# Dilated-window attention with a two-layer feed-forward: token tiles of 512, a first batch normalised after its values, and another activation sequence

## The chip, the cores and the metric

The kernel runs on one core of a Trainium2 chip. The metric is the device time of one execution in microseconds. Three runs of the kernel before gave a median of 971.6 us (lowest 970.74). The profile describes one further execution. Its engines are PE (TensorE matmul), PEld (its weight load), DVE (VectorE), ACT (ScalarE), POOL (GpSimd) and SP, which issues the DMAs.

## The reference

Eight batches of eight heads, 576 positions, head dimension 64. Heads 0 to 3 of a batch attend to the last 32 positions, heads 4 to 7 to every fourth of the last 128. The result, as 4608 tokens of 512 features, goes through two matrices with a piecewise activation between them.

```python
rel = pos[:, None] - pos[None, :]
mask_plain = (rel >= 0) & (rel < 32)
mask_dil = (rel >= 0) & (rel < 128) & (rel % 4 == 0)
scores = np.where(mask, q @ k.T / 8, -1e9); scores -= scores.max(-1)
attn = np.exp(scores); attn = attn / (attn.sum(-1) + 1e-09)
x = (attn @ v)            # to (4608, 512)
h = x @ w_in              # 512 x 2048
g = np.where(h >= 1, h, np.where(h <= -1, 0.0, (h + 1) ** 2 / 4))
out = g @ w_out           # 2048 x 512
```

## The kernel before, in words

**Precision.** Matmuls of the feed-forward run on single-pass operands. Each factor is split into a high part and a remainder (`xh`, `xl`; `gh`, `gl`; the two halves of `wi[f]`, `wo[f]`), and three products are added. The weights arrive as 64-bit words; `weights` (line 105) turns a block into its two parts with two ACT operations, one or two DVE operations, an ACT copy and a POOL subtraction. There are 16 blocks `wi` and 16 `wo`.

**Attention.** The host reorders the dilated heads so that every head is a band: six query tiles of 96 against 128 keys each. `scores` (line 169) and `scores_split` (line 198) make the scores, `reduce` (line 156) adds the mask and takes the row minimum of the negated scores, `softmax` (line 230) takes six exponentials with their sums, makes the reciprocals and multiplies on POOL. The probabilities are transposed by TensorE (`transpose_pe`, line 274; batches 0 and 1) or DVE (`transpose`, line 249; later), and `values` (line 303) multiplies two heads with their values; `store_x` (line 296) splits the result into `xh` and `xl`. Batches 0 and 1 (16 heads) take the scores in full precision ("native"); the other 48 heads use split operands (`split`, line 131).

**Feed-forward.** Tokens are cut into 12 tiles of 384. A step is one pair (token tile t, block f of 128 hidden features): `layer1` (line 345) runs 12 matmuls of 384 columns into the PSUM tile `h`, then lines 365 to 372 make `gh` and `gl`: ACT's half-and-relu, DVE's min-and-square, DVE's max with `h`, ACT's copy, and a subtraction on DVE (on POOL in the first 11 blocks). `layer2` (line 377) follows two steps later with 9 matmuls of 512 columns into three accumulators; after f = 15 they are copied and stored.

**Order.** The order of TensorE's instructions is written out by hand (line 529); on the other engines, SP's queue among them, a list scheduler orders the work by program order and simulated readiness. First come batch 0's scores, transposes and values, then a quarter of five layer-1 blocks (`partial`), then the steps. During the steps of tile 0, which this text calls the first pass, the weights are converted two blocks ahead (line 555) and `units` of batch 1's attention are put between the blocks. From step 16 on, `plan_rest` (line 408) puts a pair of heads into every six steps. PSUM has eight banks: three `acc`, two `h`, three `att`. The x tiles have four buffers each.

**Transfers.** All DMAs go through SP's queue: queries and keys of a native pair in four transfers, values one head at a time, weights at once, up to line 536.

Of the kernel before, what the change touches and what calls it, by code (L numbers as in the profile page):

```python
# [30 lines left out]
TOK = 384  # L32
# [8 lines left out]
def body(ctx, tc, q, k, v, mask, eye, w_in, w_out, out):  # L41
# [9 lines left out]
    half_t = const.tile([128, 16], F32, name="half_t")[:, :1]  # L51
# [3 lines left out]
    heads = {}  # L55

# [5 lines left out]
    def load_pair(n):  # L62

        b, h = divmod(n, H)
        if 0 < n < H:
            qr, kr = borrow(f"qr{n}")[:, :S], borrow(f"kr{n}")[:, :KPAD]
        else:
            tags = ("qs", "kk") if n % 4 else ("qr", "kr")
            qr = pool.tile([128, S], F32, tag=tags[0], name=f"qr{n}")
            kr = pool.tile([128, KPAD], F32, tag=tags[1], name=f"kr{n}")  # L70
        for j in range(2):
            r = slice(64 * j, 64 * j + 64)
            nc.sync.dma_start(out=qr[r], in_=q[b, h + j, :64])
            nc.sync.dma_start(out=kr[r], in_=k[b, h + j, :64])
            heads[n + j] = dict(qs=qr[r], ks=kr[r])

    def load(n):
        b, h = divmod(n, H)
        qr = pool.tile([128, S], F32, tag="qr", name=f"qr{n}")
        kr = pool.tile([128, KPAD], F32, tag="kr", name=f"kr{n}")  # L80
        nc.sync.dma_start(out=qr, in_=q[b, h])
        nc.sync.dma_start(out=kr, in_=k[b, h])
        heads[n] = dict(qr=qr, kr=kr)

    def load_values(n):
        if 0 < n < H:
            both = borrow(f"vt{n}")[:, : 2 * NQ * D].rearrange("p (j t d) -> p j t d", j=2, t=NQ)
        for j in range(2):
            if 0 < n < H:
                vt = both[:, j]  # L90
            else:
                vt = pool.tile([128, NQ, D], F32, tag="vt", name=f"vt{n + j}", bufs=3)
            b, h = divmod(n + j, H)
            nc.sync.dma_start(out=vt, in_=v[b, h])
            heads[n + j]["vt"] = vt
# [9 lines left out]
    def weights(f, w, name):  # L105
# [9 lines left out]
        if name == "wi":  # L115
# [12 lines left out]
        nc.scalar.copy(out=w[f][:, 0], in_=mf)  # L128
# [16 lines left out]
    banks = [("acc0", 1), ("acc1", 1), ("acc2", 1), ("h", 2), ("h", 2)]  # L145
# [10 lines left out]
    def reduce(n, t, parts):  # L156

        nc.vector.tensor_tensor_reduce(  # L158
# [10 lines left out]
    def scores(n, t0, t1):  # L169

        hd = heads[n]
        plain = n % H < H // 2
        if t0 == 0:
            begin(n)
        if n < H:
            tag, bufs = banks[(2 * n + t0 // 4) % len(banks)]
        else:
            tag, bufs = "att", 3
        sp = ps.tile([128, 512], F32, tag=tag, name=f"s{n}_{t0}", bufs=bufs)
        sv = sp[:QT, : (t1 - t0) * 128].rearrange("p (t j) -> p t j", j=128)  # L180
        if n == 0 and t0 == 0:

            half = half_t.broadcast_to([128, 128])
            for _ in range(11):
                PE.matmul(out=sp[:, :128], lhsT=half, rhs=half, start=True, stop=True)
        for t in range(t0, t1):
            PE.matmul(
                out=sv[:, t - t0],
                lhsT=hd["qs"][:, t * QT : (t + 1) * QT],
                rhs=hd["ks"][:, t * QT : t * QT + 128],  # L190
                start=True,
                stop=True,
            )
        for t in range(t0, t1):
            which = (0 if t == 0 else 2) if plain else t % 3
            reduce(n, t, (sv[:, t - t0], msk[:, which]))

    def scores_split(n, t0):
# [6 lines left out]
        sp = ps.tile([128, 512], F32, tag="att", name=f"s{n}_{t0}", bufs=3)  # L205
# [42 lines left out]

    def transpose(n):
# [9 lines left out]

    def borrow_pts():  # L260

        for i in range(2):
            for part in ("xh", "xl"):
                both = pool.tile([128, NC * TOK], F32, tag=part, name=f"pts_{part}{i}", bufs=4)
                for j in range(2):
                    pt = both[:, j * NQ * QT : (j + 1) * NQ * QT]
                    first_pts.append(pt.rearrange("p (t j) -> p t j", j=QT))

    first_pts = []

    def pt_of(n):
        return first_pts[n] if n < H else pts[n % 2]

    def transpose_pe(n):
        pt, c = pt_of(n), heads[n]["c"]
        for t0, t1 in ((0, 4), (4, NQ)):
            tag, bufs = banks[(2 * n + t0 // 4) % len(banks)] if n < H else ("att", 3)
# [5 lines left out]

    xt = {}

    def xtile(t):
        if t not in xt:
            xt[t] = (
                pool.tile([128, NC, TOK], F32R, tag="xh", name=f"xh{t}", bufs=4),
                pool.tile([128, NC, TOK], F32R, tag="xl", name=f"xl{t}", bufs=4),  # L290
# [3 lines left out]
    last = {}  # L294

    def store_x(src, t, c, dst):
        xh, xl = xtile(t)
        nc.scalar.copy(out=dst(xh[:, c]), in_=src)
        last["x"] = nc.vector.tensor_tensor(
# [3 lines left out]
    def values(n, part):  # L303
# [3 lines left out]
        odd = b % 2  # L307
        first = (2 if odd else 4) if plain else 3
        t0, t1 = ((0, first), (first, NQ))[part]
        op = ps.tile([128, 512], F32, tag="att", name=f"o{n}_{part}", bufs=3)  # L310
        for j in range(2):
            for t in range(t0, t1):
                PE.matmul(  # L313
                    out=op[64 * j : 64 * j + 64, (t - t0) * QT : (t - t0 + 1) * QT],
                    lhsT=heads[n + j]["vt"][:, t],
                    rhs=pt_of(n + j)[:, t],
# [3 lines left out]
        c = h // 2  # L320
        tok0 = b * S
        if plain:
            w = (t1 - t0) * QT
            tok = tok0 + t0 * QT
            t, at = divmod(tok, TOK)
            store_x(op[:, :w], t, c, lambda x: x[:, at : at + w])
        else:
            cut = CLS * (TOK // 2 if odd else TOK) // S
            for a, z in ((0, cut), (cut, CLS)):
                t, at = divmod(tok0 + DIL * a, TOK)  # L330
                store_x(
                    op[:, : 2 * CLS].rearrange("p (r i) -> p r i", r=2)[:, :, a:z],
                    t,
                    c,
                    lambda x: x[:, at : at + DIL * (z - a)].rearrange("p (i r) -> p r i", r=DIL)[
                        :, 2 * part : 2 * part + 2
                    ],
                )
# [6 lines left out]
    def layer1(t, f, cs=range(NC), bank=("h", 2)):  # L345
        xh, xl = xtile(t)
        if cs[0] == 0:
            hps[t, f] = ps.tile([128, 512], F32, tag=bank[0], name=f"h{t}_{f}", bufs=bank[1])[:, :TOK]
# [13 lines left out]
        y = pool.tile([128, TOK], F32, tag="y", name=f"y{t}_{f}", bufs=2)  # L362
        gh = pool.tile([128, TOK], F32R, tag="gh", name=f"gh{t}_{f}", bufs=3)
        gl = pool.tile([128, TOK], F32R, tag="gl", name=f"gl{t}_{f}", bufs=3)
        nc.scalar.activation(out=y, in_=hp, func=AF.Relu, bias=half_t, scale=0.5)  # L365
        nc.vector.scalar_tensor_tensor(out=y, in0=y, scalar=1.0, in1=y, op0=ALU.min, op1=ALU.mult)  # L366
        activated = nc.vector.tensor_tensor(out=y, in0=hp, in1=y, op=ALU.max)  # L367
        if t == 0:
            last["g", f] = activated
        nc.scalar.copy(out=gh, in_=y)  # L370
        low = nc.gpsimd if t == 0 and f < 11 else nc.vector
        low.tensor_tensor(out=gl, in0=y, in1=gh.bitcast(F32), op=ALU.subtract)  # L372
# [4 lines left out]
    def layer2(t, f):  # L377
        gh, gl = gs.pop((t, f))
        for m in range(TOK // 128):
# [12 lines left out]
            if f == NF - 1:  # L392
                o = pool.tile([128, DM], F32, tag="m", name=f"out{t}_{m}", bufs=3)
                if m == 1:
# [6 lines left out]
    nhead = B * H  # L401
    native = 2 * H

    units = []
# [3 lines left out]
    def plan_rest():  # L408

        pattern = [("0", "1"), ("2", "VW"), ("", ""), ("T3", "4"), ("5", ""), ("U", "")]  # L410

        def after(m):
            if m < nhead - 1:
                split(m + 1)
            if m < nhead - 2:
                load(m + 2)
            softmax(m)

        for p in range((nhead - native) // 2 + 1):
            n = native + 2 * p  # L420
            ops = {"V": [lambda n=n: values(n - 2, 0)], "W": [lambda n=n: values(n - 2, 1)]}
            if n < nhead:
                for j in range(2):
                    for i, u in enumerate(score_units(n + j, after)):
                        ops[str(3 * j + i)] = [u]
                ops["T"] = [lambda n=n: (transpose(n), load_values(n))]
                ops["U"] = [lambda n=n: transpose(n + 1)]
            for i, (a, b) in enumerate(pattern):
                if p == 0 and i < 3:
                    continue  # L430
                s = NF + 6 * p + i - 3
                lists = slots.setdefault(s, ([], []))
                for names, l in ((a, lists[0]), (b, lists[1])):
                    for x in names:
                        if not (p == 0 and x in "VW012"):
                            l.extend(ops.get(x, []))

    def score_units(m, after):
# [207 lines left out]
```

## Time and profile before

| quantity | value |
|---|---|
| median of three runs | 971.6 us |
| the profiled execution's own time | 971.83 us |
| its span, first to last instruction | 969.0 us |
| mean granted TensorE clock | 0.988 |
| DMA, HBM read and written | 63.49 MB, 9.44 MB |

The 2.8 us between span and time lie outside the instructions. In a group's row the columns are line, engine, operation, output from inputs, shape and count; then busy time, mean duration of one, idle time of the engine ahead of it and what ended that. A full-precision matmul has two rows in the trace, so the 48 score matmuls of batch 0 count as 96. Rows in order of time give start, duration and count.

### The profile page before, as it was taken

Reading aid. Unit: us, or ns where it says so; the run is one execution under the profiler, and the core shown is the slowest. Engines: PE = TensorE matmul, PEld = TensorE weight load, DVE = VectorE, ACT = ScalarE, POOL = GpSimd, SP = SyncE. Lnnn points to the kernel's source line nnn. Section 1 sums busy time; section 2 is a strip of 40 time slices with the busy share of each in tenths; the row PEclk is TensorE's granted clock in tenths of the full one; section 3 lists DMA queues with packets and bytes.
Section 4 is the critical chain, followed back from the end, with each engine's and each line's share of the span. In section 5 each row is a group of like instructions: output and inputs, shape, how many; then the busy total and the mean of one; then the engine's idle time right before and its main releaser. Section 6 shows DMA issues by size and latency. Waiting matters only on the chain.

```text
span 969.0 us, 15838 instructions
## 1 busy us (share of the span) xinstructions
PE 938.7 (97%) x5398; PEld 842.2 (87%) x5398; DVE 710.9 (73%) x1922; ACT 536.0 (55%) x1609; POOL 423.3 (44%) x375
## 2 busy tenths in 40 slices
PE   8779989999999999999999999999999999999998
PEld 7667768998999899999889999989899988999997
DVE  5688998878777877877787877788777777444433
ACT  6988666555565555556555545654654564322322
POOL 2566665545554554455455445545544552000000
PEclk8899999999999999999999999999999999999999
DMA  8991113213212211321222222212312310000000
GB/s 257 358 353 42 42 43 99 57 53 100 68 36 90 67 55 55 100 67 43 83 68 62 79 68 67 77 49 67 92 50 68 100 34 1 33 1 1 33 1 32
DMA packets 35888, 73.95 MB, mean 76 GB/s; under 512 B 4288, under 2 KB 12768, under 8 KB 35808
## 3 DMA queue, kind: packets, MB, share of 16 engines
q1 hardware_dynamic: 35808, 72.95, 24.1%
q8 instruction: 42, 0.69, 0.3%
q14 instruction: 38, 0.31, 0.1%
HBM read 63.49 MB, written 9.44 MB: 75 GB/s over the span
## 4 chain that ended last, share of the span: by engine, by line
PE 73%; DVE 12%; ACT 7%; DMA 4%; SPq 2%; POOL 2%; issue 1%; POOLq 0%; DVEq 0%; ACTq 0%
PE h L352 34%; PE acc L385 33%; DVE y L366 3%; PE s L208 3%; PE o L313 3%; ACT c L233 3%; DMA wi_raw<-w_in 2%; DVE pt L255 2%; DVE wo_m L123 2%; DVE y L367 1%; DMA kr<-k_in 1%; DVE gl L372 1%; ACT gh L370 1%; DVE c L241 1%; ACT y L365 1%
## 5 line engine op out<-in xcount | busy, mean ns | idle before, releaser
L352 PE MATMUL h<-xh,wi 128*128 128x384 f32 x1536 | 431.5, 342 | 6.1 <-DVE y L367 5.1
L385 PE MATMUL acc<-wo,gh 128*128 128x512 f32 x1152 | 390.1, 393 | 3.0 <-DVE out L395 3.0
L352 PEld LDWEIGHTS h<-xh,wi 128*128 128x128 f32 x1536 | 282.7, 189 | 15.7 <-DVE y L367 5.3
L352 PE MATMUL h<-xl,wi 128*128 128x384 f32 x768 | 259.7, 338 | 0.0
L385 PEld LDWEIGHTS acc<-wo,gh 128*128 128x128 f32 x1152 | 216.8, 188 | 45.0 <-DVE out L395 4.3
L370 ACT CAST gh<-y 128x384 fp32r<-128x384 f32 x192 | 98.4, 512 | 270.8 <-DVE y L367 270.8
L226 POOL TENSOR_TENSOR c<-c,msk 96x256 f32<-96x256 f32 (+1 forms) x168 | 116.6, 700 | 300.8 <-ACT c L216 300.5
L385 PE MATMUL acc<-wo,gl 128*128 128x512 f32 x576 | 225.9, 392 | 0.0
L366 DVE SCALAR_TENSOR_TENSOR y<-y 128x384 f32<-128x384 f32 x192 | 137.4, 716 | 73.5 <-ACT y L365 72.7
L365 ACT ACTIVATE y<-h,half_t 128x384 f32<-128x384 f32 x192 | 111.2, 579 | 114.8 <-PE h L352 114.1
L372 DVE TENSOR_TENSOR gl<-y,gh 128x384 fp32r<-128x384 f32 x181 | 120.9, 668 | 53.8 <-ACT gh L370 52.1
L233 ACT ACTIVATE c<-c 96x128 f32<-96x128 f32 x384 | 151.3, 397 | 13.3 <-DVE c L158 12.7
L352 PEld LDWEIGHTS h<-xl,wi 128*128 128x128 f32 x768 | 144.9, 189 | 4.1
L255 DVE STREAM_TRANSPOSE pt<-c 32x192 f32<-32x192 f32 x288 | 106.1, 368 | 24.7 <-POOL c L245 20.6
L385 PEld LDWEIGHTS acc<-wo,gl 128*128 128x128 f32 x576 | 108.4, 188 | 15.6 <-POOL gl L372 0.2
L245 POOL TENSOR_TENSOR c<-c 96x768 f32<-96x768 f32 x64 | 98.4, 1537 | 50.1 <-DVE c L244 43.8
L158 DVE CUSTOM_DVE_ANT_0 c<-s,c 96x128 f32<-96x128 f32 x288 | 73.1, 283 | 61.2 <-POOL c L226 56.0
L367 DVE TENSOR_TENSOR y<-h,y 128x384 f32<-128x384 f32 x192 | 107.1, 558 | 6.5
L140 POOL TENSOR_TENSOR kk<-kr,kk 128x608 fp32r<-128x608 f32 x48 | 81.5, 1698 | 3.8
L137 POOL TENSOR_TENSOR qs<-qr,qs 64x576 fp32r<-64x576 f32 x48 | 71.2, 1482 | 5.9 <-issue 2.3
L233 ACT ACTIVATION_READ_ACCUMULATOR c<-c 96x1 f32 x384 | 73.3, 191 | 0.0
L241 DVE SCALAR_TENSOR_TENSOR c<-c 96x6 f32<-96x6 f32 x64 | 62.4, 976 | 7.0 <-ACT c L233 5.9
(47 smaller groups left out, 726.7 us busy)
## 6 DMA issues: line engine op xcount, KB each, us to landing
kr<-k_in SPq DMA_DIRECT2D x48, 304.0 KB, 3.1
qr<-q_in SPq DMA_DIRECT2D x48, 288.0 KB, 2.8
vt<-v_in SPq DMA_DIRECT2D x64, 192.0 KB, 3.0
out<-out SPq DMA_DIRECT2D x36, 256.0 KB, 2.1
wi_raw<-w_in SPq DMA_DIRECT2D x16, 512.0 KB, 9.2
wo_raw<-w_in SPq DMA_DIRECT2D x16, 512.0 KB, 10.2
kr<-k_in SPq DMA_DIRECT2D x16, 152.0 KB, 4.0
qr<-q_in SPq DMA_DIRECT2D x16, 144.0 KB, 3.9
```

Source lines behind the costliest of these rows:

```text
L140: nc.gpsimd.tensor_tensor(out=kk[:, 1], in0=hd["kr"], in1=kk[:, 0].bitcast(F32), op=ALU.subtract)
L226: nc.gpsimd.tensor_tensor(out=c[:, ts], in0=c[:, ts], in1=m, op=ALU.add)
L233: nc.scalar.activation(out=c[:, t], in_=c[:, t], func=AF.Exp, bias=st[:, 0, t : t + 1], scale=-1.0, accum_out=st[:, 1, t : t + 1],)
L245: nc.gpsimd.tensor_tensor(out=c, in0=c, in1=st[:, 2].unsqueeze(2).broadcast_to([QT, NQ, 128]), op=ALU.mult)
L255: nc.vector.transpose(out=pt[r : r + 32, :, 32 * g : 32 * g + 32], in_=c[32 * g : 32 * g + 32, :, r : r + 32],)
L352: PE.matmul(out=hp, lhsT=wi[f][:, w, 128 * c : 128 * c + 128], rhs=x[:, c], start=c == 0 and i == 0, stop=c == NC - 1 and i == len(terms) - 1,
L365: nc.scalar.activation(out=y, in_=hp, func=AF.Relu, bias=half_t, scale=0.5)
L366: nc.vector.scalar_tensor_tensor(out=y, in0=y, scalar=1.0, in1=y, op0=ALU.min, op1=ALU.mult)
L367: activated = nc.vector.tensor_tensor(out=y, in0=hp, in1=y, op=ALU.max)
L370: nc.scalar.copy(out=gh, in_=y)
L372: low.tensor_tensor(out=gl, in0=y, in1=gh.bitcast(F32), op=ALU.subtract)
L385: PE.matmul(out=acc[m], lhsT=g[:, r], rhs=wo[f][:, w], start=f == 0 and i == 0, stop=f == NF - 1 and i == len(terms) - 1,)
```

## The change

- `TOK` is 512: 9 token tiles, 144 steps, 12 + 12 matmuls of 512 columns per step. PSUM is now four `acc`, two `h`, two `att`; batch 0 also uses the four `acc` banks by turns. The x tiles have three buffers.
- The activation is a DVE clamp of `h` to [-1, 1], an ACT square of (y + 1) / 2, a DVE max written back into `h`, an ACT copy of `h` to `gh` and a DVE subtraction from `h`; `y` has one buffer, `gh` and `gl` two.
- Batch 0 takes no sums with its exponentials. POOL subtracts the minima, ACT takes one exponential per head, and in `values` TensorE sums the transposed probabilities against a column of ones, DVE makes the reciprocals, TensorE spreads them over 64 partitions (a matmul with the identity), ACT copies them out and DVE multiplies them in.
- The scores of two native heads are made alternately, one from partitions 0 to 63 and the other from 64 to 127.
- The first four `wi` blocks and `wo` 0 are converted with DVE in place of ACT for part of the work.
- Queries, keys and values of a native pair come in one transfer each; weight blocks are fetched four (`wo`) and six (`wi`) steps ahead. SP's queue is in program order too.
- The hand-written order is one table of half steps (`slots`): a native pair every seven half steps, from head 16 on a pair every eight (four steps). The third score set of a split head directly follows the second.

```diff
-TOK = 384
+TOK = 512
...
+    banks = [("acc0", 1), ("acc1", 1), ("acc2", 1), ("acc3", 1)]
...
+        for t in range(t0, t1):
+            for m, sv in zip(pair, svs):
+                PE.matmul(
+                    out=sv[:, t - t0],
+                    lhsT=heads[m]["qs"][:, t * QT : (t + 1) * QT],
...
+    def exponentials(n):
+        least = st[:, 0].unsqueeze(2).broadcast_to([QT, NQ, 128])
+        nc.gpsimd.tensor_tensor(out=c, in0=c, in1=least, op=ALU.subtract)
+        last["act"] = nc.scalar.activation(out=c, in_=c, func=AF.Exp, scale=-1.0)
...
+        if n < H:
+            for i in range(2 * NQ):
+                PE.matmul(
+                    out=sums[:, i : i + 1],
+                    lhsT=pt_of(n + i // NQ)[:, i % NQ],
+                    rhs=one_t,
...
+            nc.vector.tensor_scalar(out=inv, in0=sums, scalar1=EPS, scalar2=None, op0=ALU.add)
+            nc.vector.reciprocal(out=inv, in_=inv)
+        for part in range(2):
+            op = ps.tile([128, 512], F32, tag="att", name=f"o{n}_{part}", bufs=2)
...
+                        PE.matmul(
+                            out=sc[64 * j : 64 * j + 64, i * QT : (i + 1) * QT],
+                            lhsT=inv[:, at : at + 1].broadcast_to([QT, 64]),
+                            rhs=ident,
...
+                nc.scalar.copy(out=over, in_=sc[:, w])
+                nc.vector.tensor_tensor(out=op[:, w], in0=op[:, w], in1=over, op=ALU.mult)
...
-        nc.scalar.activation(out=y, in_=hp, func=AF.Relu, bias=half_t, scale=0.5)
-        nc.vector.scalar_tensor_tensor(out=y, in0=y, scalar=1.0, in1=y, op0=ALU.min, op1=ALU.mult)
-        activated = nc.vector.tensor_tensor(out=y, in0=hp, in1=y, op=ALU.max)
-        nc.scalar.copy(out=gh, in_=y)
-        low = nc.gpsimd if t == 0 and f < 11 else nc.vector
-        low.tensor_tensor(out=gl, in0=y, in1=gh.bitcast(F32), op=ALU.subtract)
+        nc.vector.tensor_scalar(
+            out=y, in0=hp, scalar1=-1.0, scalar2=1.0, op0=ALU.max, op1=ALU.min
+        )
+        nc.scalar.activation(out=y, in_=y, func=AF.Square, bias=half_t, scale=0.5)
+        activated = nc.vector.tensor_tensor(out=hp, in0=hp, in1=y, op=ALU.max)
+        copied = nc.scalar.copy(out=gh, in_=hp)
+        nc.vector.tensor_tensor(out=gl, in0=hp, in1=gh.bitcast(F32), op=ALU.subtract)
...
+    for n in range(H, native, 2):
+        u = 7 * (n - H) // 2
+        place(u, lambda n=n: scores_pair(n, 0, 4))
+        place(u + 1, lambda n=n: (scores_pair(n, 4, NQ), after_pair(n)))
+        place(u + 5, lambda n=n: transpose_pe(n))
+        place(u + 6, lambda n=n: transpose_pe(n + 1))
+        place(u + 7, lambda n=n: values_native(n))
+    for n in range(native, nhead, 2):
+        u = 27 + 4 * (n - native)
+        for j, at in ((0, u), (1, u + 4)):
+            place(at, lambda m=n + j: scores_split(m, 0))
+            place(at + 1, lambda m=n + j: scores_split(m, 2))
+            place(at + 1, lambda m=n + j: (scores_split(m, 4), after(m)))
+        place(u + 4, lambda n=n: (transpose(n), load_values(n)))
+        place(u + 8, lambda n=n: transpose(n + 1))
+        place(u + 11, lambda n=n: values(n))
...
+            if s + 6 < NF:
+                fetch(s + 6, w_in, "wi")
+            if s + 4 < NF:
+                fetch(s + 4, w_out, "wo")
+            if 0 < s < NF:
+                todo = [("wo", s, False)]
+                if s + 3 < NF:
+                    todo.append(("wi", s + 3, False))
+                behind(last["g", max(s - 2, 0)], *todo)
+            if s < 2:
+                layer1(*steps[s], range(2, NC))
+            elif s < len(steps):
+                layer1(*steps[s])
+            run(2 * s)
+            while l2 <= s - lag and l2 < len(steps):
+                layer2(*steps[l2])
+                l2 += 1
+            run(2 * s + 1)
```

More of the change, by code (lines that the diff above doesn't have):

```diff
@@ L40, in body @@
 @with_exitstack
-def body(ctx, tc, q, k, v, mask, eye, w_in, w_out, out):
+def body(ctx, tc, q, k, q2, k2, v, mask, eye, w_in, w_out, out):
     nc = tc.nc
@@ L62, in load_pair @@
     def load_pair(n):
-        b, h = divmod(n, H)
         if 0 < n < H:
@@ L114, in weights @@
         )
-        if name == "wi":
+        if name == "wi" and not on_vector:
             top = raw.bitcast(U8).rearrange("p (n x) -> p n x", x=8)[:, :, 3]
@@ L167, in reduce, with scores_pair @@
         )
-    def scores(n, t0, t1):
-        hd = heads[n]
+    def scores_pair(n, t0, t1):
+        pair = (n, n + 1)
         plain = n % H < H // 2
[L173 to L185, printed above, removed]
-        for t in range(t0, t1):
[L187 to L196, printed above, removed]
+        svs = []
+        for m in pair:
+            if t0 == 0:
+                begin(m)
+            tag, bufs = bank(n)
+            sp = ps.tile([128, 512], F32, tag=tag, name=f"s{m}_{t0}", bufs=bufs)
+            svs.append(sp[:QT, : (t1 - t0) * 128].rearrange("p (t j) -> p t j", j=128))
+            if m == 0 and t0 == 0:
+                half = half_t.broadcast_to([128, 128])
+                for _ in range(11):
+                    PE.matmul(out=sp[:, :128], lhsT=half, rhs=half, start=True, stop=True)
+        for t in range(t0, t1):
+            for m, sv in zip(pair, svs):
+                PE.matmul(
+                    out=sv[:, t - t0],
+                    lhsT=heads[m]["qs"][:, t * QT : (t + 1) * QT],
+                    rhs=heads[m]["ks"][:, t * QT : t * QT + 128],
+                    start=True,
+                    stop=True,
+                )
+        for m, sv in zip(pair, svs):
+            for t in range(t0, t1):
+                which = (0 if t == 0 else 2) if plain else t % 3
+                reduce(m, t, (sv[:, t - t0], msk[:, which]))
     def scores_split(n, t0):
@@ L204, in scores_split @@
         c = hd["c"]
-        sp = ps.tile([128, 512], F32, tag="att", name=f"s{n}_{t0}", bufs=3)
+        sp = ps.tile([128, 512], F32, tag="att", name=f"s{n}_{t0}", bufs=2)
         sv = sp[:QT].rearrange("p (t a j) -> p t a j", t=2, a=2)
@@ L258, in transpose @@
                 )
+    first_pts = []
     def borrow_pts():
[L262 to L269, printed above, removed]
+        for part in ("xh", "xl"):
+            both = pool.tile([128, NC * TOK], F32, tag=part, name=f"pts_{part}", bufs=3)
+            for j in range(3):
+                pt = both[:, j * NQ * QT : (j + 1) * NQ * QT]
+                first_pts.append(pt.rearrange("p (t j) -> p t j", j=QT))
     def pt_of(n):
-        return first_pts[n] if n < H else pts[n % 2]
+        return first_pts[n] if n < len(first_pts) else pts[n % 2]
     def transpose_pe(n):
@@ L319, in values @@
                 )
[L320 to L338, printed above, removed]
+            inv = heads[n + 1]["st"].rearrange("p k t -> p (k t)")[:, NQ:]
```

324 lines of the change are left out of this document (148 added, 176 removed).

## The prediction

> **What bounds the kernel now.** I read the page first, then the busy time by stage, then TensorE's waits, then its rows in order of time.
>
> ```profile
> PE 938.7 (97%) x5398; PEld 842.2 (87%) x5398; DVE 710.9 (73%) x1922; ACT 536.0 (55%) x1609; POOL 423.3 (44%) x375
> PE   8779989999999999999999999999999999999998
> PEclk8899999999999999999999999999999999999999
> ```
>
> TensorE is 97% busy; its only thin slices are the first five or six, where the granted clock is lower too. Busy time by stage separates them:
>
> ```profile
> 0.00:51.00 51.00, 41.10 (x301) 37.25 (x302) 31.61 (x145) 40.53 (x143) 21.05 (x20) 0.83 0.96 313
> 51.00:162.00 111.00, 97.34 (x580) 82.29 (x579) 97.95 (x239) 82.07 (x239) 72.51 (x56) 0.97 0.32 104
> 162.00:966.00 804.00, 800.28 (x4521) 722.66 (x4519) 581.32 (x1539) 413.44 (x1229) 329.71 (x301) 1.00 0.19 57
> ```
>
> (Columns: stage, length, then PE, PEld, DVE, ACT, POOL, clock, DMA.) There are three regimes: the start (batch 0's attention; ACT 40.5 of 51 us), the first pass (16 blocks of the first token tile, with 32 weight conversions and batch 1's attention; DVE 98 of 111), and the rest, where PE is busy 800 of 804. The rest can only shrink by shorter matmul streams; the first two by moving work off DVE and ACT, or by giving their idle PE more to do. After 150 us PE's waits hold one line:
>
> ```profile
> PE acc L385 <- DVE out L395: 3.0, 3, 1.2
> ```
>
> **The matmul stream.** In the undisturbed tail one step is twelve 384-column matmuls, then nine of 512:
>
> ```profile
> 861.18 0.34 PE L352 MATMUL h<-xh,wi 128*128 128x384 f32 x1
> ...
> 863.28 0.40 PE L385 MATMUL acc<-wo,gh 128*128 128x512 f32 x1
> ...
> 865.34 0.34 PE L352 MATMUL h<-xh,wi 128*128 128x384 f32 x1
> ```
>
> From start to start: 2.10 us / 12 = 0.175 us for 384 columns, 2.06 / 9 = 0.229 for 512. The extra 128 columns cost 0.054, so 384 should cost 0.162 if there were no fixed part; each matmul carries some 13 ns. With 512 tokens a step is twelve and twelve: 24 x 0.2285 = 5.48 us, and there are 144 steps for 192. Layer 1 falls from 192 x 2.10 = 403 to 144 x 2.74 = 395; layer 2 keeps its 1728 matmuls. That alone is 8 us.
>
> "TensorE: Matmul & The Clock Gate" in the Trainium skill, section "Back-to-back issue gap", gives an isolated warm matmul N/2.4 + 2.5 ns: 162.5 ns for 384 and 216 for 512, and by it the saving would be 1.5 us, an estimate that speaks against the change. The rows show 175 and 229, so I keep mine.
>
> **The rest of the kernel.** I cut at the end of layer 2's block 15, the row at 161.24:
>
> ```profile
> 161.24 0.34 PE L352 MATMUL h<-xh,wi 128*128 128x384 f32 x1
> ...
> 964.87 0.39 PE L385 MATMUL acc<-wo,gh 128*128 128x512 f32 x1
> ```
>
> From there to 965.2 are 804 us, in them 174 layer-1 blocks and 176 of layer 2: 365 + 363 = 728. The other 76 us are attention of heads 17 to 63 and its seams. After the change 126 + 128 blocks remain, 254 x 2.74 = 696; with the same 76 and 4 us of tail, the span ends **776 us after that cut**. So every extra token of the first pass is work moved ahead of the cut, into a regime where PE had idle time.
>
> Do the other engines keep up? Per block the change has clamp, square, max, copy, subtract, on 512 columns:
>
> ```profile
> L366 DVE SCALAR_TENSOR_TENSOR y<-y 128x384 f32<-128x384 f32 x27 | 15.1, 560 | 50.4 <-ACT y L365 50.4
> L367 DVE TENSOR_TENSOR y<-h,y 128x384 f32<-128x384 f32 x26 | 14.5, 558 | 0.9
> ...
> L395 DVE COPY out<-acc 128x512 f32<-128x512 f32 x1 | 0.7, 680 | 0.0
> ```
>
> (DVE in the tail.) A 512-column DVE operation out of PSUM takes 0.68; three are 2.05 us per 5.48 us step, where three of 0.56 stood per 4.16. A DVE write into PSUM (the new max) is in no row; I bound it by 0.56 (this max at 384 columns) and 1.36, twice the copy, and take 0.69 as nearest to the copy. At 1.36 DVE would still have room. On ACT:
>
> ```profile
> L397 ACT COPY out<-acc 128x512 f32<-128x512 f32 x24 | 13.8, 587 | 3.4 <-PE acc L385 3.2
> L128 ACT CAST wi<-wi_m 128x512 fp32r<-128x512 f32 x16 | 9.9, 628 | 2.8 <-DVE wi_m L123 2.5
> ```
>
> square 0.63 and copy 0.59. The chain from a finished h to gl is 0.68 + 0.63 + 0.69 + 0.59 + 0.68, some 3.5 us with hand-overs. h now stays held through the subtract, but its next writer comes three blocks (8.2 us) later; gh's second buffer is free one block (2.7 us) after the step, when the copy is due anyway. Both hide behind PE's stream; without that cover each microsecond late would cost 144 us in all. Pairs of heads now come every four steps (22 us of GEMM) in place of six (25), so attention is denser, but DVE's share per pair falls with the activation.
>
> The scores are the tight spot: "att" has two buffers in place of three, and the third score set of a head follows the first after one block and one set, 2.74 + 0.24 = 3.0 us. Before:
>
> ```profile
> 407.49 0.40 PE L208 MATMUL s<-kk,qs 128*96 128x256 f32 x2
> ```
> ```profile
> 408.58 0.35 ACT L216 COPY c<-s 96x256 f32<-96x256 f32 x1
> ```
> ```profile
> 409.01 0.99 POOL L226 TENSOR_TENSOR c<-c,msk 96x256 f32<-96x256 f32 x1 [3.41 <-ACT c L216]
> ```
> ```profile
> 411.14 0.28 DVE L158 CUSTOM_DVE_ANT_0 c<-s,c 96x128 f32<-96x128 f32 x1
> ```
>
> That set was read out 3.9 us after its issue, of which waiting in ACT's queue took some 0.7 and in DVE's, behind an activation, 0.9. In the new order the set starts when the block's subtract is nearly through and before the next clamp, so I expect about 2.3 us and no wait; bounds 0 and 0.9 us for 47 heads, 0 to 42 us. I take 0, and put the far end with a rival.
>
> **The first pass.** What DVE did in it:
>
> ```profile
> L366 DVE SCALAR_TENSOR_TENSOR y<-y 128x384 f32<-128x384 f32 x18 | 28.0, 1557 | 5.4 <-ACT y L365 5.3
> L123 DVE SCALAR_TENSOR_TENSOR wo_m<-wo_m,wo_raw 128x512 uint32<-128x512 uint32 x13 | 18.5, 1424 | 0.0
> ...
> L367 DVE TENSOR_TENSOR y<-h,y 128x384 f32<-128x384 f32 x18 | 10.0, 557 | 0.6
> ...
> L372 DVE TENSOR_TENSOR gl<-y,gh 128x384 fp32r<-128x384 f32 x6 | 4.6, 759 | 0.2 <-ACT gh L370 0.2
> ```
>
> The reader is to see 1557 against 560 ns: the same instruction, all of whose operands lie in SBUF, takes nearly three times as long here, where POOL is busy 72 of 111 us, while the max, which reads PSUM, takes 557 in both places. The change gives each of the three an operand in PSUM. DVE's activation falls from 28.0 + 10.0 + 4.6 = 42.6 to 18 x 3 x 0.69 = 37 us although the tile is a third larger and eleven subtractions come over from POOL. So DVE needs 98 - 42.6 + 37 = 92 us, and with 5 for weight conversions that now fall later about 97.
>
> PE's need from two finished layer-1 blocks to the cut: 16 + 16 blocks x 2.74 = 88; batch 1's attention by
>
> ```profile
> 98.23 1.55 PE L187 MATMUL s<-kr,qr 64*96 64x128 f32 x12
> 99.71 0.45 PE L352 MATMUL h<-xh,wi 128*128 128x384 f32 x1
> ...
> 89.41 1.59 PE L313 MATMUL o<-pt,vt 128*64 128x96 f32 x24
> 90.93 0.44 PE L352 MATMUL h<-xh,wi 128*128 128x384 f32 x1
> ```
>
> 96 score rows x 0.123 = 12, 96 value rows x 0.063 = 6, transposes and head 16 some 6. The new order alternates two heads that lie in different halves of the partitions; no row shows whether their matmuls overlap. I bound the scores by 12 and, at the value rows' pitch, 6 us, and take 12: **112 us**. By "TensorEngine Tiling (Array Packing)" of the Trainium skill, "Key Properties", tiles on separate row groups run in parallel, so the scores would take half and the forecast would be 6 us lower; no run here shows it.
>
> Before, PE had 91 us of work in the 111 us after 50.4: 20 us of waits. With DVE at 97 of 117 (it was 98 of 111) and PE the fuller engine, I take 5 us of waits, bounds 2 and 20.
>
> **The start.** Batch 0 now subtracts the minimum on POOL, takes one exponential per head, sums on TensorE and scales after the values.
>
> ```profile
> L233 ACT ACTIVATE c<-c 96x128 f32<-96x128 f32 x384 | 151.3, 397 | 13.3 <-DVE c L158 12.7
> L245 POOL TENSOR_TENSOR c<-c 96x768 f32<-96x768 f32 x64 | 98.4, 1537 | 50.1 <-DVE c L244 43.8 <-ACT wo_m L112 2.1 <-DVE c L158 1.2
> L136 ACT CAST kk<-kr 128x608 fp32r<-128x608 f32 x48 | 33.7, 701 | 0.0
> L158 DVE CUSTOM_DVE_ANT_0 c<-s,msk 96x128 f32<-96x128 f32 x96 | 21.5, 278 | 9.0 <-PE s L187 9.0
> ```
>
> ACT loses 48 exponentials (151.3 / 384 = 0.39 each, 19 us) and gains eight wide ones (0.85 each by the 608-column cast) and eight copies of 288 columns (0.38 each by the score copy's 0.35 for 256): 9 us less. DVE gains eight multiplies, at most 0.56 each by the 384-column max, and loses four pairs of small operations; those 4 us lie under its idle time (31.6 of 51 busy). POOL's subtractions follow the reductions; the last of eight ends near 9.4 + 8 x 1.5 = 21 us, and the last exponential at 22, where the last normalisation came here:
>
> ```profile
> 30.61 1.47 POOL L245 TENSOR_TENSOR c<-c 96x768 f32<-96x768 f32 x1 [1.16 <-DVE c L244]
> ```
> ```profile
> 7.24 0.29 DVE L158 CUSTOM_DVE_ANT_0 c<-s,msk 96x128 f32<-96x128 f32 x1 [6.37 <-PE s L187]
> ```
> ```profile
> 30.13 0.71 PE L280 MATMUL t<-ident,c 96*128 96x96 f32 x6
> ...
> 50.05 0.34 PE L352 MATMUL h<-xh,wi 128*128 128x384 f32 x1
> ```
> ```profile
> wi_raw<-w_in SPq DMA_DIRECT2D x16, 512.0 KB, 9.2
> wo_raw<-w_in SPq DMA_DIRECT2D x16, 512.0 KB, 10.2
> ```
>
> That stall goes, and PE is late next: 24 more matmuls per pair, 48 rows x 0.063 = 3 us, 12 in all, with each scale waiting for DVE's reciprocal; DVE's reductions start at 7.2 as before, behind the warm-up matmuls, and take 21.5 / 96 = 0.22 each. From the end of the reductions (7.2 + 48 x 0.22 = 17.8): transposes 6.5 (48 rows at 0.12, and hand-over), four values-with-sums at 4.5, two half blocks 2.7, the last store 2.5 and the last quarters 1.4 make 49 us to two finished blocks; 45 to 55 if waits fall otherwise. Before, one block and four quarters, as much, were done at 50.4. Transfers: one DMA replaces two or four, and weights are fetched four to six steps ahead, 20 us and more, against 10 us to land; I cost them at nothing.
>
> **The sum.** 49 + 112 + 5 = 166 at the cut; + 776 = 942 span. The profiled run took 971.83 for a span of 969.0, so + 2.8: **945 us**, against the median of 971.6 that this profile stands beside.
>
> **Rivals.** (a) The first pass stays held by queues of DVE and ACT: waits of 20 us as before, 960. For: ACT chains hand over four times per block. Against: DVE's inflated row is gone. 0.13. (b) The start gets longer: ten more microseconds from the serial sum, reciprocal, scale on a cold PE (clock 0.83 there), 955. 0.07. (c) The first pass doesn't use its slack but grows with its tokens: 50.4 + 111 x 4/3 = 198, + 776 + 3 = 977, the change does not do what it says. Against: more than half of DVE's 98 us there are per head or per weight, not per token. 0.05. (d) The other side: the two "att" buffers. If the first set takes longer than 3.0 us to be read out, PE stops in front of each third set; at 0.9 us for 47 heads 987, slower than before from 0.6 us a head. For: 3.9 us before. Against: DVE and ACT are emptier at that moment. 0.07.
>
> **How the numbers follow.** Forecast 0.68, from 932 (scores overlapped, waits 2, start 45) to 955. The range 931 to 963 adds (a) and (b) and leaves out (c), (d) and the far tails, some 2 in 10. Faster by over 2% (below 952, about what a measurement of this kernel tells from no change): nearly all of the forecast and a little of (a), (b): 0.68. Slower by over 2%: (d), 0.07. Within: 0.25.
>
> **What would show it.** Right: pitch 0.229 in both layers; clamp, max and subtract near 0.69 in the first pass too; layer 2's block 15 ending at 160 to 170; PE over 99% after it. Wrong: PE waits on DVE before scores (d), a cut behind 180 (a, c), or layer 1 starting in full after 55 (b).

## The result: 1010.6 us, 4% slower

The changed kernel took 1010.62 us (median of 4 runs, 1010.03 to 1011.14) against 971.38 for the kernel before on the same chip: ratio 1.0406, 95% interval 1.0386 to 1.0426. One of the four runs of the kernel before took 2337.5 us and is left out of the ratio. The forecast of 945 us lies 66 us below.

The page of the changed kernel, its totals and two rows of its forty slices:

```profile
PE 954.5 (95%) x5014; PEld 770.3 (76%) x5014; DVE 649.0 (64%) x1821; ACT 510.7 (51%) x1434; POOL 385.5 (38%) x364
PE   7978988999999999999999999999999999999998
PEclk8778999999999999999999999999999999999999
```

DVE did lose work (649 us for 711), but TensorE's is no shorter (954.5 for 938.7, although the streams should have shrunk), and its share fell. Busy time by stage, cut where the forecast cut it: at the end of the second finished block (here about 66.5) and of layer 2's block 15 (198.9). The columns are PE, PEld, DVE, ACT, POOL, clock, DMA share and GB/s:

```profile
0.00:66.50 66.50, 55.54 (x501) 48.91 (x502) 38.06 (x183) 29.28 (x68) 18.51 (x17) 0.79 0.50 188
66.50:198.90 132.40, 116.35 (x615) 92.37 (x614) 92.70 (x234) 88.85 (x235) 64.05 (x49) 0.94 0.33 118
198.90:1005.00 806.10, 782.65 (x3901) 629.05 (x3899) 517.89 (x1405) 392.59 (x1134) 302.99 (x298) 1.00 0.18 56
```

The start is 15 us longer than before and at a lower clock (0.79 for 0.83). The first pass is 21 us longer, at 0.94 for 0.97. The rest is as long as before, 806 for 804 us, though less of the matrix streams is left for it (254 blocks of 2.76 us, 701, for 728): TensorE now stands still for 23 us of it, where it did for 4. What it waited for, over the whole span (total, times, longest):

```profile
PE s L218 <- DVE xl L314: 20.8, 20, 2.1
PE s L196 <- DVE xl L314: 5.5, 4, 2.6
PE s L196 <- DVE c L167: 5.5, 8, 2.5
PE s L218 <- DVE c L167: 5.1, 15, 1.9
```

Nearly all of it is score sets (`s`); a further 3.3 us, ahead of the native set at 147.34, stand in the same list without a releaser (`issue`). In the largest line a set waits for `xl`, the subtraction that empties the values' `o` tiles. One such place, in order of time on TensorE and then on DVE:

```profile
419.71 1.43 PE L344 MATMUL o<-pt,vt 128*64 128x96 f32 x24
...
425.06 0.45 PE L218 MATMUL s<-kk,qs 128*96 128x256 f32 x2 [0.96 <-DVE xl L314]
```
```profile
421.08 0.42 DVE L314 TENSOR_TENSOR xl<-o,xh 128x256 fp32r<-128x256 f32 x1 [0.52 <-ACT xh L313]
421.42 2.27 DVE L272 STREAM_TRANSPOSE pt<-c 32x192 f32<-32x192 f32 x6
423.73 0.70 DVE L417 TENSOR_TENSOR h<-h,y 128x512 f32<-128x512 f32 x1
424.46 0.56 DVE L314 TENSOR_TENSOR xl<-o,xh 128x288 fp32r<-128x288 f32 x2
```

The two `o` tiles hold both `att` buffers. The score set comes only half a step (12 matmuls) later, while on DVE six transposes and a maximum stand ahead of the last subtractions, so the second buffer is free only at 425.0. In the first pass the native pairs' scores stand directly behind the `o` tiles, with nothing between:

```profile
82.05 1.43 PE L344 MATMUL o<-pt,vt 128*64 128x96 f32 x24
86.13 0.46 PE L196 MATMUL s<-kr,qr 64*96 64x128 f32 x2 [2.65 <-DVE xl L314]
87.25 1.99 PE L196 MATMUL s<-kr,qr 64*96 64x128 f32 x14 [0.67 <-DVE xl L314]
89.17 0.79 PE L399 MATMUL h<-xh,wi 128*128 128x512 f32 x1
```

and behind that wait the granted clock is halved. TensorE by single microseconds; the columns are stretch, length, busy time with its instructions, granted clock, DMA share and GB/s:

```profile
86.00:87.00 1.00, 0.46 (x2) 0.94 0.00 0
87.00:88.00 1.00, 0.75 (x7) 0.50 0.00 0
...
93.00:94.00 1.00, 1.00 (x4) 0.64 0.00 0
94.00:95.00 1.00, 1.00 (x11) 1.00 0.00 0
```

Some 3.3 us of waiting are followed by 6.8 us at half clock (from 86.9 to 93.7). The block of layer 1 that ran there took 5.0 us (89.17 to 94.2) where 2.79 is its time.

### The profile page after: what moved, and what is told of

It is laid out like the page before. It is cut to its first block, busy times and chain, and to the rows that moved or that the text cites. A ratio compares the mean times of both kernels' runs of the same rounds, so it can differ in the third digit from the quotient of the medians.

```text
span 1008.4 us, 14918 instructions
## 1 busy us (share of the span) xinstructions
PE 954.5 (95%) x5014; PEld 770.3 (76%) x5014; DVE 649.0 (64%) x1821; ACT 510.7 (51%) x1434; POOL 385.5 (38%) x364
## 4 chain that ended last, share of the span: by engine, by line
PE 57%; DVE 19%; ACT 13%; issue 5%; POOL 4%; DMA 2%; SPq 0%; DVEq 0%; POOLq 0%; ACTq 0%
PE h L399 27%; PE acc L434 21%; DVE pt L272 9%; ACT c L243 4%; POOL c L255 3%; DVE h L417 3%; PE o L344 3%; PE s L218 3%; DVE c L251 3%; ACT y L415 2%; DVE xl L314 2%; ACT qs L136 1%; ACT kk L137 1%; ACT gh L418 1%; ACT c L226 1%
## 5 line engine op out<-in xcount | busy, mean ns | idle before, releaser
L399 PE MATMUL h<-xh,wi 128*128 128x512 f32 x1152 | 391.2, 400 | 3.4 <-ACT xh L313 2.1
L399 PEld LDWEIGHTS h<-xh,wi 128*128 128x128 f32 x1152 | 219.7, 191 | 54.0 <-ACT xh L313 2.5
L399 PE MATMUL h<-xl,wi 128*128 128x512 f32 x576 | 229.3, 398 | 0.0
L415 ACT ACTIVATE y<-y,consts 128x512 f32<-128x512 f32 x144 | 104.2, 724 | 143.0 <-DVE y L412 143.0
L412 DVE TENSOR_SCALAR y<-h 128x512 f32<-128x512 f32 x144 | 98.7, 686 | 80.5 <-PE h L399 80.5
L418 ACT CAST gh<-h 128x512 fp32r<-128x512 f32 x144 | 84.0, 583 | 113.2 <-DVE h L417 65.6
L421 DVE TENSOR_TENSOR gl<-h,gh 128x512 fp32r<-128x512 f32 x144 | 97.2, 675 | 53.4 <-ACT gh L418 52.5
L417 DVE TENSOR_TENSOR h<-h,y 128x512 f32<-128x512 f32 x144 | 100.5, 698 | 36.2 <-ACT y L415 33.6
L218 PE MATMUL s<-kk,qs 128*96 128x256 f32 x288 | 56.4, 289 | 26.7 <-DVE xl L314 20.8
L313 ACT CAST xh<-o 128x288 fp32r<-128x288 f32 (+8 forms) x112 | 38.4, 379 | 83.3 <-PE o L344 51.0
L218 PEld LDWEIGHTS s<-kk,qs 128*96 128x96 f32 x288 | 40.9, 161 | 48.4 <-issue 38.9
```

What stands on the lines that cost most here:

```text
L218: PE.matmul(out=sv[:, t - t0], lhsT=hd["qs"][:, t * QT : (t + 1) * QT], rhs=hd["ks"][:, :, t * QT : t * QT + 128], start=True, stop=True,)
L399: PE.matmul(out=hp, lhsT=wi[f][:, w, 128 * c : 128 * c + 128], rhs=x[:, c], start=c == 0 and i == 0, stop=c == NC - 1 and i == len(terms) - 1,
L412: nc.vector.tensor_scalar(out=y, in0=hp, scalar1=-1.0, scalar2=1.0, op0=ALU.max, op1=ALU.min)
L415: nc.scalar.activation(out=y, in_=y, func=AF.Square, bias=half_t, scale=0.5)
L417: activated = nc.vector.tensor_tensor(out=hp, in0=hp, in1=y, op=ALU.max)
L418: copied = nc.scalar.copy(out=gh, in_=hp)
```

## The experiments

**Theory A**, from these views: the time went where scores stand behind the `o` tiles with two `att` buffers, and in the first pass the halved clock adds to it; whatever is left lies in the start. **Theory B**, the rival: DVE and ACT are simply behind; move one wait and another opens.

For each kernel a mark was read on ACT: the first copy of a finished output tile, which ends the first pass.

```profile
161.89 0.58 ACT L397 COPY out<-acc 128x512 f32<-128x512 f32 x1
```
```profile
197.03 0.59 ACT L446 COPY out<-acc 128x512 f32<-128x512 f32 x1 [1.84 <-PE acc L434]
```

(Before, then after.) "Rest" is the profiled span less this mark. The table has all kernels that ran; the sections below say what they are.

| kernel | time, us | ratio to before, 95% | first copy | rest |
|---|---|---|---|---|
| before | 971 | 1 | 161.9 | 807.1 |
| changed | 1010.6 | 1.0386 to 1.0426 | 197.0 | 811.4 |
| x1 native values later | 991.7 | 1.0181 to 1.0243 | 181.4 | 811.1 |
| x2 split values earlier | 993.8 | 1.0195 to 1.0248 | 198.3 | 795.1 |
| x3 both | 976.2 | 1.0034 to 1.0076 | 176.8 | 794.8 |
| x5 changed, softmax first | 996.3 | 1.0249 to 1.0279 | 184.0 | 811.0 |
| x6 both, softmax first | 964.4 | 0.9922 to 0.9955 | 167.9 | 795.1 |
| x9 both, sums by ones | 977.4 | 1.0054 to 1.0084 | 180.9 | 795.1 |
| x10 x6, old activation | 998.6 | 1.0265 to 1.0304 | 173.5 | 822.7 |
| x11 x6, split transfers | 965.7 | 0.9929 to 0.9959 | 171.0 | 794.7 |
| x12 x6, heads in turn | 964.8 | 0.9908 to 0.9942 | 167.7 | 795.5 |
| x7 before, clamp and square | 987.4 | 1.0159 to 1.0190 | 154.6 | 830.7 |
| x8 before, two buffers | 987.5 | 1.0150 to 1.0180 | 169.2 | 816.0 |
| x13 changed, waits filled | 1004.5 | 1.0305 to 1.0349 | 193.3 | 811.5 |

### Moving the values away from the scores (x1, x2, x3)

x1 puts the native pairs' values two half steps later, x2 the split heads' values one half step earlier, x3 does both; nothing else changes.

```diff
-        place(u + 7, lambda n=n: values_native(n))
+        place(u + 9, lambda n=n: values_native(n))
...
-        place(u + 11, lambda n=n: values(n))
+        place(u + 10, lambda n=n: values(n))
```

Expected of x1: 

> Only the values of batch 1 move, two half steps later (after the next pair's scores in place of directly ahead of them). Theory A (the two att buffers): each of four seams in the first pass now costs a wait of 3 us and the half clock behind it, 15 to 20 us in all, so 990 to 996 us and no wait of PE's native scores on the x stores. Theory B (waits are a symptom, the next one takes their place; the loss is the added TensorE work of the start): 1006 or more.

Expected of x2: 

> Only the values of heads 16 to 63 move, one half step earlier, away from the next score set. Theory A: the 21 us of waits of the split scores on the x stores go, 985 to 992 us. Theory B: the values now wait for the score sets ahead of them as long, 1003 to 1012.

Expected of x3: 

> Both moves. Theory A: the gains add, 965 to 976 us. Theory B: 1000 or more.

Measured: 991.7, 993.8 and 976.2 us, that is 19, 17 and 34 below the changed kernel. x1's gain is all in the first pass (197.0 to 181.4), x2's all in the rest (811.4 to 795.1), and x3 has both. TensorE's waits in x3:

```profile
PE s L218 <- DVE c L167: 7.3, 28, 0.5
...
PE s L218 <- DVE xl L314: 1.6, 1, 1.6
```

The waits for `xl` are gone but for one of 1.6 us; what is left is the third score set behind the first (28 times 0.26 us). Theory B falls. In time x1 lies in A's range, x2 came out 2 us above it, and x3 at its upper end.

### The wait or the clock behind it (x13)

Sixteen matmuls of constants, which nobody reads, stand in the changed kernel ahead of the three native score sets that follow `o` tiles.

```diff
+        if n > H and t0 == 0:
+            fill = ps.tile([128, TOK], F32, tag="h", name=f"fill{n}", bufs=2)
+            half = half_t.broadcast_to([128, 128])
+            for _ in range(16):
+                PE.matmul(out=fill[:, :128], lhsT=half, rhs=half, start=True, stop=True)
```

Expected: 

> The changed kernel with 16 matmuls of constants, whose result nobody reads, ahead of each of the three native score sets that stand directly behind a pair of o tiles (heads 10, 12, 14): they run where TensorE waits for the o tiles to be read, so that the wait stays, but not the idleness. Theory R (of the 15.7 us that moving the values took from the first pass, about half is the clock halved behind the wait): 1001 to 1007 us, and the block of layer 1 behind the second seam at 2.8 to 3.5 us in place of 5.0. Theory S (the wait itself is all of it): 1009 to 1014 us.

Measured: 1004.5 us (1000.6 to 1006.6 in 5 runs). The same place on TensorE:

```profile
84.20 1.43 PE L349 MATMUL o<-pt,vt 128*64 128x96 f32 x24
85.56 3.84 PE L198 MATMUL fill<-consts 128*128 128x128 f32 x32
89.33 1.12 PE L201 MATMUL s<-kr,qr 64*96 64x128 f32 x16
90.37 0.51 PE L404 MATMUL h<-xh,wi 128*128 128x512 f32 x1
```

From the start of `o` to the bulk of the scores it is 5.1 us, as in the changed kernel (82.05 to 87.25, 5.2), but 3.8 us of them are now full of useless work; the clock stays at 1.00 at all three places, and the block behind takes 3.0 us in place of 5.0. So work that does nothing makes the kernel 6 us faster by the medians (3.6 by the profiled spans, 1004.8 for 1008.4). The spans hold other differences too, so the three places are better compared one by one: from the start of the values to the end of the block behind the scores they take 9.15, 9.11 and 9.15 us for 12.17, 9.58 and 10.51, which is 4.9 us less. At the second and third the filling is longer than the wait was, by 1.1 and 0.4 us (4.05 and 4.76 us from the start of the values to the bulk of the scores in the changed kernel, 5.12 here), so an estimate of the clock's part is 4.9 + 1.4 = 6.3 us. TensorE's idle time at the three places was 8.8 us (2.65 and 0.67, 0.49 and 1.68, 3.33), and the two together, 15.1, are nearly the 15.7 us by which x1 shortens the first pass. Theory R holds: the wait itself is the larger share, and the clock behind it some four tenths.

### The start: who normalises the first batch (x5, x6, x9)

x5 gives the first batch its softmax back in the changed kernel, x6 in x3; the sums, scale matmuls, copies and multiplications behind the values go.

```diff
-        if n < H:
+        if False:
...
-        exponentials(n)
-        exponentials(n + 1)
+        softmax(n)
+        softmax(n + 1)
```

Expected of x5: 

> The changed kernel with the first batch's heads normalised by softmax again (48 exponentials on ACT with their sums, one reciprocal and one POOL multiplication a head), and no sums, scale matmuls, copies and multiplications behind the values; everything else as changed. Theory C (the sums and scales, at half clock and in a chain over TensorE, DVE and ACT, are what makes the start late): 996 to 1004 us, and the cut comes over 5 us earlier. Theory D (the exponentials put back on ACT cost the start as much as they save): 1008 to 1018 us.

Expected of x6: 

> The kernel with both placements moved (976 us) and the first batch by softmax again. Theory C: the start gains here what it gains in the changed kernel, 960 to 970 us, under the kernel before. Theory D: 973 to 984 us.

Measured: 996.3 and 964.4 us, 14 and 12 less; the first copy comes 13.0 and 9.0 us earlier, the rest is unchanged. Theory C. x6 is faster than both kernels, 0.6% below the one before. Groups of TensorE instructions of the changed kernel up to 67 us (busy time, mean ns), and one pair's values in order of time:

```profile
L357 PE MATMUL r<-ident,c 96*64 96x96 f32 x96 | 10.3, 322 | 0.1
...
L330 PE MATMUL sums<-consts,pts_xh 128*96 128x1 f32 x36 | 5.1, 271 | 0.0
```
```profile
21.19 3.89 PE L330 MATMUL sums<-consts,pts_xh 128*96 128x1 f32 x24
25.01 1.28 PE L344 MATMUL o<-pts_xh,vt 128*64 128x96 f32 x10
...
29.18 1.21 PE L296 MATMUL t<-ident,c 96*128 96x96 f32 x12
```

What such a row takes from start to start depends on the granted clock: a row of one column took 0.16 us at a clock of 0.50 (24 from 21.19 to 25.01) and 0.085 at 1.00 (24 from 48.42 to 50.47), a row of the values, with 96 columns, 0.10 and 0.06 (ten each from 25.01 and from 50.47). The scales are 10.3 us of TensorE's busy time, the sums of all eight heads 11.0, some of it shared with the values' rows among which they stand, and this pair's values took 8.0 us (21.19 to 29.18). The fourth pair took 4.5; the columns are as in the table by stage:

```profile
21.19:29.18 7.99, 7.99 (x74) 7.86 (x73) 3.24 (x9) 3.04 (x6) 2.02 (x2) 0.52 1.03 402
48.42:52.91 4.49, 4.49 (x73) 4.36 (x72) 2.24 (x6) 0.69 (x2) 1.26 (x1) 1.00 0.00 0
```

At a clock of 0.52 the same work takes 1.8 times as long. In x6 a pair is:

```profile
23.91 2.35 PE L344 MATMUL o<-pts_xh,vt 128*64 128x96 f32 x24
26.18 1.21 PE L296 MATMUL t<-ident,c 96*128 96x96 f32 x12
```

2.3 us. The first layer-1 block of the first pass ends at 57.8 in the changed kernel and at 45.2 in x6.

x9 keeps the new way but takes the sums straight in the values' layout, by 64 columns of ones, with one wide reciprocal:

```diff
-                            lhsT=inv[:, at : at + 1].broadcast_to([QT, 64]),
-                            rhs=ident,
...
+                        lhsT=one_t.broadcast_to([128, 64]),
+                        rhs=pt_of(n + j)[:, 3 * part : 3 * part + 3].rearrange("p t j -> p (t j)"),
...
-                nc.scalar.copy(out=over, in_=sc[:, w])
+                nc.vector.reciprocal(out=over, in_=sc[:, w])
```

Expected: 

> The kernel with both placements moved; the first batch's sums come straight in the layout of the values, from matmuls with 64 columns of ones (4 of 288 columns a pair in place of 24), and one DVE reciprocal a part takes the place of the small reciprocal, the scale matmuls and the ACT copy. Theory F (what makes the start late is the chain of hops behind the values, TensorE to DVE to TensorE to ACT to DVE): 955 to 970 us. Theory G (the start waits for the exponentials and transposes ahead of it, whatever the chain): 972 to 980 us.

Measured: 977.4 us, in theory G's range and no better than x3 (976.2), with the first copy 4 us later. But that does not decide between the theories, since DVE, in its groups up to 66 us, shows a price nobody had reckoned with:

```profile
L349 DVE RECIPROCAL over<-r 128x288 f32<-128x288 f32 x8 | 15.6, 1950 | 5.4 <-PE r L341 5.4
```

Eight reciprocals of 288 columns cost 15.6 us. Whether fewer hops alone would help stays open.

### The activation, in both orders (x7, x10)

x7 puts clamp and square into the kernel before; x10 takes them out of x6.

```diff
-        nc.scalar.activation(out=y, in_=hp, func=AF.Relu, bias=half_t, scale=0.5)
-        nc.vector.scalar_tensor_tensor(out=y, in0=y, scalar=1.0, in1=y, op0=ALU.min, op1=ALU.mult)
+        nc.vector.tensor_scalar(
+            out=y, in0=hp, scalar1=-1.0, scalar2=1.0, op0=ALU.max, op1=ALU.min
+        )
+        nc.scalar.activation(out=y, in_=y, func=AF.Square, bias=half_t, scale=0.5)
```

Expected of x7: 

> The kernel before with the new activation alone: DVE clamp from PSUM and ACT square in place of ACT relu and DVE minimum-times-itself; tiles of 384, three buffers, the old order. Theory H (VectorE's operation with two SBUF operands, 1557 ns in the first pass, holds nothing that TensorE waits for): 968 to 973 us, with that line at 0.5 to 0.6 us in the first pass. Theory I (it holds the first pass): 955 to 966 us.

Expected of x10: 

> The kernel with both placements moved and the first batch by softmax (964 us) with the old activation (ACT relu, DVE minimum-times-itself, DVE maximum). Theory J (the clamp and the square, one change of engine more, cost the later passes here what they cost in the kernel before, where the time after the first pass grew from 807 to 831 us): 945 to 957 us, the part after the first pass 5 to 20 us shorter. Theory K (a step of 5.5 us covers the hop; the first pass loses the 7 us that the clamp gained in the kernel before): 966 to 974 us, the part after the first pass still at 795 us.

Both expectations failed. x7 took 987.4 us: its first pass is 7.3 us shorter, as theory I has it, but its rest is 23.6 us longer. x10 took 998.6 us: the old activation costs 34 us there, 5.6 in the first pass and 27.6 in the rest. TensorE's waits of x10, over the whole span:

```profile
PE s L218 <- DVE c L167: 27.9, 26, 2.1
```

This is the third score set behind the first, at 1.07 us each. How it comes about, on DVE and POOL around one such set (it started at 422.65, 0.88 us late):

```profile
416.54 1.89 DVE L413 SCALAR_TENSOR_TENSOR y<-y 128x512 f32<-128x512 f32 x1 [0.27 <-ACT y L412]
418.35 1.12 DVE L272 STREAM_TRANSPOSE pt<-c 32x192 f32<-32x192 f32 x3
419.50 0.70 DVE L414 TENSOR_TENSOR h<-h,y 128x512 f32<-128x512 f32 x1
420.23 1.14 DVE L272 STREAM_TRANSPOSE pt<-c 32x192 f32<-32x192 f32 x3
...
422.01 0.28 DVE L167 CUSTOM_DVE_ANT_0 c<-s,c 96x128 f32<-96x128 f32 x1
```
```profile
416.41 1.47 POOL L255 TENSOR_TENSOR c<-c 96x768 f32<-96x768 f32 x1 [0.38 <-DVE c L254]
```

The instruction with two operands in SBUF takes 1.89 us while POOL works (the next one, at 423.82, took 0.69, and POOL stood still until 424.12); everything behind it on DVE is late, and the reduction that frees the first set's buffer starts at 422.01. So in the new order, with two buffers, the new activation is worth 34 us. For x7, DVE and ACT alternate once more per block, and TensorE's idle time from 200 to 900 us grows from 3.0 to 16.3, spread over seven lines of waits, of which the largest is `PE o L313 <- ACT c L216` with 3.6. Why the hop costs that much in the old order was not settled.

### Two buffers in the old order (x8)

```diff
-        sp = ps.tile([128, 512], F32, tag="att", name=f"s{n}_{t0}", bufs=3)
+        sp = ps.tile([128, 512], F32, tag="att", name=f"s{n}_{t0}", bufs=2)
```

and so at the four other places that name `att`. Expected: 

> The kernel before with two att buffers in place of three, all else as it was. Theory A (what costs is a score set directly behind the o tiles of the values; the old order has half a step or more between them): 971 to 982 us. Theory Q (with two buffers the wait comes in any order): 987 us or more.

Measured: 987.5 us, 16.5 above before and in theory Q's range: 7.3 in the first pass, 8.9 in the rest. So theory A's claim that the order alone decides is too strong: the third buffer was worth something in the old order too, though in the rest about half of what the changed order paid (16.3).

### What turned out not to matter (x11, x12)

x11 cuts x6's q and k transfers back into halves; x12 issues a pair's score matmuls one head after the other.

```diff
-        nc.sync.dma_start(out=qr, in_=q[n // 2])
...
+            nc.sync.dma_start(out=qr[r], in_=q[n // 2][r])
...
```
```diff
-        for t in range(t0, t1):
-            for m, sv in zip(pair, svs):
+        for m, sv in zip(pair, svs):
+            for t in range(t0, t1):
```

Expected of x11: 

> The 964 us kernel with each of the pairs' q and k transfers cut back into two halves of 64 partitions, in the same order of use. Theory M (the merged transfers bring the start forward): 968 to 980 us, first scores later. Theory N (the transfers are behind the scores' own work either way): 963 to 966 us.

Expected of x12: 

> The 964 us kernel with the score matmuls of a pair issued one head after the other in place of alternating. Theory O (alternating heads, on the two halves of the rows, overlap: 24 matmuls took 1.55 us, where the kernel before took 7.97 for 72): 967 to 972 us. Theory P (the time between scores is set by VectorE's reductions, and the matmuls' own rate is hidden): 963 to 966 us.

Measured: 965.7 and 964.8 for x6's 964.4: theories N and P. Yet the rows of alternating heads do follow each other faster; the start of x6 and of x12 on TensorE:

```profile
5.70 1.55 PE L196 MATMUL s<-kr,qr 64*96 64x128 f32 x24
```
```profile
5.91 7.10 PE L196 MATMUL s<-kr,qr 64*96 64x128 f32 x72
```

65 ns a row for alternating heads, 99 in turn, at a granted clock of 1.00 in both. In x6 TensorE then waits for the reductions (0.62 us at 7.88), so the gain is not seen.

## Why the prediction was wrong, point by point

**The step that failed is the paragraph on the two `att` buffers.** It looked at one successor only, the third score set behind the first, took no wait, and put the far end, 42 us, with rival (d). It never asked which instruction comes behind the two `o` tiles of the values, although the change's list of places puts native scores in the same half step and split scores one half step later. That costs 16.3 us in the rest (x2) and 15.7 in the first pass (x1). Rival (d) had the resource and the side right, but another successor: its own wait came to 5.1 us in the changed kernel, and to 27.9 only with the old activation (x10). By the prediction's own signs a cut behind 180 spoke for (a) or (c). TensorE's idle time in the first pass was indeed 16 us (132.40 less 116.35), but it was not the queues as such: with the values moved and as much work on DVE and ACT (92.5 and 89.8 us busy for 92.7 and 88.9), x6's first pass takes 117.7 us (52.0 to 169.7), 7.2 of them idle, where 112 + 5 were forecast.

**The 49 us to two finished blocks were mis-sized.** The terms were 48 rows at 0.063 for sums and scales of a pair and 4.5 us for each pair's values. The four pairs took 8.0, 6.1, 7.7 and 4.5 us, 26.3 for 18, at granted clocks of 0.52, 0.72, 0.60 and 1.00. The one pair at full clock took just what was forecast, so it is the clock of this stretch that the term left out, more than the work. That is 8.3 of the 17.5 us by which the start came out longer; most of the others are the first native score sets, which stand ahead of the second block (57.79 to 64.24) and which the prediction had counted behind the start, and a wait of 2.1 us for `xh` at 55.99. The slow pairs are rival (b), which named the cold clock and had 0.07; x5 prices the sums and scales at 13.0 us of the time to the first copy.

**That extra tokens go where TensorE had idle time left out the clock.** The 20 us of waits before were 13.7 us of idle time by the prediction's own row by stage (111.00 less 97.34). A wait in the first pass costs more than its length: 3.3 us of it were followed by 6.8 at half clock, and x13 shows that keeping TensorE busy alone wins 6 us by the medians. "TensorE: Matmul & The Clock Gate" of the Trainium skill, section "HAM oscillation — how this bites in real kernels", has the same mechanism: a wait that crosses the activity window lets the next burst start cold, each time. The trace agrees: the values ended at 83.5 and the clock fell at 86.9, some 3.4 us later, the length that the section names, and in between TensorE was busy for 0.46 us only.

**Two small terms.** A step is 5.52 us, not 5.48:

```profile
851.84 0.39 PE L434 MATMUL acc<-wo,gh 128*128 128x512 f32 x1
...
854.57 0.40 PE L399 MATMUL h<-xh,wi 128*128 128x512 f32 x1
...
857.36 0.39 PE L434 MATMUL acc<-wo,gh 128*128 128x512 f32 x1
```

2.73 / 12 = 0.2275 in layer 2 and 2.79 / 12 = 0.2325 in layer 1: 144 steps of 5.52 us are 795 where 192 of 4.16 were 799, so the streams save 4 us, not 8. (Of the two pitches that the prediction weighed, 0.216 from "TensorE: Matmul & The Clock Gate" of the Trainium skill, section "Back-to-back issue gap", and the row's 0.229, the row was right.) From the cut to the span's end x6 takes 793.3 us where 776 were forecast: 254 blocks x 0.02 more are 5.1, TensorE's idle time above the old 3.7 another 6.3; 5.9 stay unassigned.

**What held.** DVE's operations in the first pass, each with an operand in PSUM, and ACT's square:

```profile
L412 DVE TENSOR_SCALAR y<-h 128x512 f32<-128x512 f32 x18 | 12.3, 685 | 10.8 <-PE h L399 10.8
L417 DVE TENSOR_TENSOR h<-h,y 128x512 f32<-128x512 f32 x17 | 11.8, 696 | 6.9 <-ACT y L415 6.9
...
L421 DVE TENSOR_TENSOR gl<-h,gh 128x512 fp32r<-128x512 f32 x17 | 11.5, 675 | 4.8 <-ACT gh L418 4.7
```
```profile
L415 ACT ACTIVATE y<-y,consts 128x512 f32<-128x512 f32 x18 | 13.0, 722 | 12.3 <-DVE y L412 12.3
```

685, 696 and 675 ns against 0.69, with no inflation beside POOL; the square took 0.72 against 0.63. That the activation's order of engines would hide behind TensorE's stream held in the new order; x7 shows that it does not in every order. Transfers at nothing held (x11), and so did taking no gain from alternating heads (x12): "TensorEngine Tiling (Array Packing)" of the Trainium skill, "Key Properties", is borne out in part by the rows, 65 ns for 99 where half would be 50, but not in the time.

**The sum, remade.** 166 at the cut became 198.9. Of the 33 us the native values' place is 15.7 and the sums and scales 13.0; x6, without either, has its cut at 169.7. The rest became 809.5: x6's 793.3 and x2's 16.3. The plan was worth 964 us with its two placements moved and the first batch's softmax kept, not 945.

## What to carry to other kernels

When a pool of buffers shrinks, list every user of it in issue order and ask of each what frees its buffer and how far back that is on the slower engine's queue; one harmless pair proves nothing about the others. Work moved onto the engine that is the bound should be priced by its instruction count, since here a row of one column cost no less than one of 96 (0.085 us for 0.06), and at the clock of the stretch that it goes to. And where the clock falls behind a stop, a stop of 3.3 us can cost nearly its own length again (3.0 us at the first place of x13), so a place in the order that avoids the stop is worth more than the trace of waits says.

## What the runs showed of the hardware that was not expected

- A DVE reciprocal of 128 x 288 took 1950 ns, the multiplication of the same size beside it 456 (x9).
- In the 3.4 us up to 86.9 TensorE was busy for 0.46 us, and the granted clock was then halved for 6.8 us. The length of one stop alone does not decide: of two stops of 2.10 us in the changed kernel, the one that ended at 55.99 was followed by 3.4 us at half clock (56.1 to 59.5), the one that ended at 175.98 by none, and the stops in the rest, up to 1.43 us, lowered it nowhere. The clock can be low without stops, too: between 25 and 50 us of the changed kernel, in the stretch of transposes, sums and scales, TensorE was busy for 24.86 of 25 us at 0.72:

```profile
25.00:50.00 25.00, 24.86 (x249) 23.29 (x248) 14.51 (x39) 9.22 (x23) 5.10 (x4) 0.72 0.34 133
```

- Writing a DVE result into PSUM cost next to nothing extra: the maximum took 696 ns there, the subtraction into SBUF 675.
